# A retention layer and a gated MLP on one core: blocks of 256 rows, quarters of the array, a written program order

## The chip, the cores and the metric

The kernel runs on one core of a Trainium2 chip. A core has a matrix engine (TensorE; PE in the profile, its weight loads PEld), three engines for element-wise work (VectorE, DVE; ScalarE, ACT; GpSimd, POOL), and SyncE (SP), which here only issues DMAs. Each engine takes its instructions from its own queue in order, and waits in that queue for what other engines must have finished. The metric is the device time of one execution in microseconds (us); less is better. All times below are in us unless marked ns.

## The reference

Eight batches of 576 rows pass through a retention layer of eight heads of 64, and then through a gated MLP with a spatial gate (a mixing of the 576 rows with each other).

```python
scores = scale * np.matmul(q, k.transpose(0, 1, 3, 2))      # q, k, v: 8 x 8 x 576 x 64
gamma = 1.0 - 2.0 ** (-5.0 - np.arange(H))
Dmat = np.where(rel >= 0, gamma[:, None, None] ** rel, 0.0) # rel = t - s
x = np.matmul(scores * Dmat, v)                             # -> 8 x 576 x 512
h = gelu(x @ w_in)                                          # 512 -> 1024, tanh form
u, v = h[..., :512], h[..., 512:]
v_n = (v - mean) / np.sqrt(var + 1e-06) * g_ln              # over the 512 columns
v_s = np.einsum('ts,bsd->btd', w_sg, v_n) + b_sg[None, :, None]
out = x + (u * v_s) @ w_out                                 # float32
```

## The kernel before

The decay gamma^(t-s) splits into a factor of the row t and one of the row s, so the retention runs as a linear recurrence over chunks of rows: inside a chunk the masked scores (`sc`, then `ret`) are multiplied with the values, and what came before enters through a 64x64 state for each head (`zp` in PSUM, its copy `zbd` in SBUF).

The 4608 rows are cut into 36 chunks of 128. Two batches form a pair of nine chunks (`NT`); the middle chunk (`MID`, the fifth) holds the last 64 rows of one batch and the first 64 of the next. Queries, keys and values come in float32 with one row a partition, in pieces of 64 numbers (256 bytes). For each chunk:

- `load` (L67) issues the DMAs on SP; `prep` (L172) casts q and k to bfloat16 (L176) and multiplies v by its decay factor (L178), both on POOL.
- `attn_T` (L184) transposes q and k on PE, two heads on top of each other; DVE copies `qT` (L191), and ACT (L193) and DVE (L194) put the two heads of k into the halves of a zero-padded tile `kbd`, so that a whole 128x128 array computes the scores of one head.
- `attn_S` (L197) computes the scores and DVE multiplies them by the triangular mask (L208).
- `attn_O` (L212) sums the carried part (L223) and the local part (L228) in PSUM, each with half of the array's columns; DVE multiplies by the row's decay from the table `ttab` and writes `xT` (L231), which has the columns of x on the partitions.
- `attn_Z` (L234) adds to the state; DVE (L247) and ACT (L248) copy its diagonal blocks into `zbd`.
- `mlp_V` (L254): four matmuls of 512 columns (`hv`, L258), gelu on ACT (`vg`, L261), mean and variance on DVE (L263, L265), 1/sqrt(var) and -mean/sqrt(var) on POOL (L267, L268, L270), and the normalised `vn` on ACT (L272).
- `mlp_U` (L275): sixteen matmuls (`hu`, L282) and gelu into `uT` (L285).

For a batch whose five chunks of `vn` are there, `mlp_W` (L287) mixes the rows: for each of four groups of columns and each half of 288 rows five matmuls (`wp`, L295). DVE applies g and b in one instruction (`vs`, L301) and multiplies by `uT` in a second one (`gT`, L304). Then for each chunk `mlp_O` (L306) does the last matmuls (L311), adds x through a matmul with the identity (L314), copies to SBUF (`ob`, L317), and issues the output DMA from ACT's queue (L318).

The loop at L354 names the order of this work: for step i the scores of chunk i, the MLP of chunk i-1, the transposes of chunk i+1, and two waiting pieces of `mlp_W` and `mlp_O` a step. A planner may still reorder each engine's queue by data and priorities. PSUM has eight banks: one each for transposes, `ot` and the state, two for scores, three (`psD`) for `hv`, `hu`, `wp` and `op`.

Of the kernel before, what the change touches and what calls it, by code (L numbers as in the profile page):

```python
# [19 lines left out]
def kernel(  # L20
# [18 lines left out]
    NP = B // 2  # L39
# [11 lines left out]
    vnp = ctx.enter_context(tc.tile_pool(name="vnp", bufs=14))  # L51
# [5 lines left out]
    def segs(m):  # L57

        if m < MID:
            return [(0, 0, 128 * m, 128)]  # L60
        if m == MID:
            return [(0, 0, 128 * m, S - 128 * m), (S - 128 * m, 1, 0, 128 * (m + 1) - S)]
        return [(0, 1, 128 * m - S, 128)]
# [3 lines left out]
    def load(i):  # L67
        p, m = divmod(i, NT)
        qk = ld.tile([128, 2, H, D], F32, name="qk", tag="qk")
        vf = ld.tile([128, H, D], F32, name="vf")  # L70
        for (p0, b, r0, n) in segs(m):
            bb = 2 * p + b
            nc.sync.dma_start(qk[p0:p0 + n, 0, :, :], q[bb, :, r0:r0 + n, :].transpose([1, 0, 2]))
            nc.sync.dma_start(qk[p0:p0 + n, 1, :, :], k[bb, :, r0:r0 + n, :].transpose([1, 0, 2]))
            nc.sync.dma_start(vf[p0:p0 + n, :, :], v[bb, :, r0:r0 + n, :].transpose([1, 0, 2]))
        loaded[i] = (qk, vf)

    load(0)

# [5 lines left out]
    g_col = consts.tile([128, KK], F32, name="g_col")  # L85
    w_stage = []
    for half in (1, 0):
        for c in (0, 2):
            wst = ld.tile([128, 2, F2], F32, name="wst", tag="qk")
            nc.sync.dma_start(wst[:], moe_w_in.rearrange("(c p) f -> p c f", p=128)[:, c:c + 2, half * F2:(half + 1) * F2])  # L90
            w_stage.append((half, c, wst))
        load(1 if half else 2)
    nc.sync.dma_start(b_bc[:], moe_b_sg.partition_broadcast(128))
    nc.sync.dma_start(g_col[:], moe_g_ln.rearrange("(c p) -> p c", p=128))


    ident = consts.tile([128, 128], BF, name="ident")
    make_identity(nc, ident[:])
    tri = consts.tile([128, 128], BF, name="tri")
    nc.gpsimd.memset(tri[:], 1.0)  # L100
# [306 lines left out]
```

## Time and profile before

| | |
|---|---|
| Median of three runs | 277.83 us (277.71 to 278.25) |
| Span of the profiled execution, first to last instruction | 276.5 us |
| Busy: PE / DVE / ACT / POOL | 232.7 / 197.4 / 128.1 / 121.9 us |
| Moved by DMA | 41.75 MB in 120,670 packets, 113,792 of them under 512 bytes |
| Mean granted TensorE clock | 0.963 |

The page gives the profiled execution by its span alone, which is 1.3 us under the median of the runs; a sum of its rows is a sum for the span. In a row of a group stand the line, the engine, the operation, out<-in with shapes, the count, then the busy time of the group and the mean ns of one, and after the second bar the idle time of the engine just before them with what ended it. In a row of the timeline stand the start and the length of a run of equal instructions. Matmuls are pipelined: one lasts about 0.22 us from start to end while the next may start after a quarter of that, so a rate is read from starts, and a busy PE isn't a PE at its peak.

### The profile page before, as it was taken

To read this page: it belongs to the slowest core of one execution; us is meant where nothing else is said; L and a number is where in the kernel's file an instruction comes from. 1 tells how busy PE (TensorE), PEld (TensorE's weight loads), DVE (VectorE), ACT (ScalarE), POOL (GpSimd) and SP (SyncE) were. 2 spreads that over 40 slices of the span, in tenths; PEclk is the share of its full clock that TensorE was granted. 3 is DMA by queue.
4 is the path that set the end of the run, shared out by engine and by line. 5 is a ranking of instruction groups with operands and counts; after the bars stand their busy time and mean duration, and the time that the engine had idled before them with its cause. 6 is when DMAs were issued, how large, how long until landed. Compare 5 with 4: busy or idle time off the path is not lost.

```text
span 276.5 us, 6611 instructions
## 1 busy us (share of the span) xinstructions
PE 232.7 (84%) x2626; PEld 167.1 (60%) x2626; DVE 197.4 (71%) x446; ACT 128.1 (46%) x226; POOL 121.9 (44%) x204
## 2 busy tenths in 40 slices
PE   0376894989999889988899799888997999989794
PEld 0234663666757666666666566666666776666562
DVE  4444663579997898569966996679876975698170
ACT  3441443242446445563455355562555456644603
POOL 4924417057445364546625485364555551111200
PEclk9995797599999999999999999999999999999999
DMA  8999899987005899879829996999658002200214
GB/s 173 256 280 207 163 210 202 223 162 163 10 2 146 205 211 202 185 161 244 162 92 225 183 209 154 210 187 181 147 148 195 0 27 90 78 2 2 78 76 190
DMA packets 120670, 41.75 MB, mean 151 GB/s; under 512 B 113792, under 2 KB 114880, under 8 KB 120640
## 3 DMA queue, kind: packets, MB, share of 16 engines
q1 hardware_dynamic: 114272, 30.71, 55.7%
q10 hardware_dynamic: 5184, 9.44, 9.2%
q0 software_dynamic: 1184, 1.19, 2.5%
q8 instruction: 20, 0.33, 0.5%
q14 instruction: 10, 0.08, 0.1%
HBM read 33.08 MB, written 9.44 MB: 154 GB/s over the span
## 4 chain that ended last, share of the span: by engine, by line
DVE 41%; PE 25%; ACT 10%; DMA 7%; issue 6%; POOL 6%; ACTq 2%; SPq 2%; POOLq 0%; DVEq 0%
DVE ret L208 8%; DVE vs L301 8%; DVE gT L304 7%; DMA wst<-in_moe_w_in_dram 6%; DVE bst L263 5%; PE op L311 5%; DVE xT L231 5%; ACT ob L317 5%; PE hv L258 4%; PE hu L282 4%; PE wp L295 3%; ACT vg L261 3%; PE tp L189 2%; ACTq L318 2%; POOL rs L268 2%
## 5 line engine op out<-in xcount | busy, mean ns | idle before, releaser
L267 POOL TENSOR_SCALAR rs<-mv 128x1 f32<-128x1 f32 x36 | 8.0, 223 | 113.3 <-DVE mv L265 106.1
L272 ACT ACTIVATE vn<-vg,nm,rs 128x512 bf16<-128x512 f32 x36 | 29.3, 814 | 52.3 <-POOL nm L270 52.3
L282 PE MATMUL hu<-xT,w_in 128*128 128x128 bf16 x576 | 40.5, 226 | 6.5 <-DVE w_in L349 3.2
L208 DVE TENSOR_TENSOR ret<-sc,tri 128x512 bf16<-128x512 f32 x64 | 40.9, 680 | 6.1 <-PE sc L206 6.0
L263 DVE BATCH_NORM_STATS2 bst<-vg 128x6 f32<-128x512 f32 x36 | 24.7, 687 | 27.6 <-ACT vg L261 27.6
L176 POOL CAST qkb<-qk 128x1024 bf16<-128x1024 f32 x36 | 37.5, 1041 | 14.6 <-DMA qk<-in_k_dram 9.6
L295 PEld LDWEIGHTS <-vn 128*128 128x128 bf16 x320 | 30.0, 97 | 20.3 <-issue 13.0
L258 PE MATMUL hv<-w_in,xT 128*128 128x512 bf16 x144 | 39.9, 399 | 2.7 <-DVE xT L231 2.5
L282 PEld LDWEIGHTS <-w_in 128*128 128x128 bf16 x576 | 36.3, 101 | 9.5 <-issue 4.8
L311 PE MATMUL op<-w_out,gT 128*128 128x512 bf16 x144 | 37.2, 379 | 0.0
L261 ACT ACTIVATE vg<-hv 128x512 f32<-128x512 f32 x36 | 21.5, 596 | 28.1 <-PE hv L258 22.1
L301 DVE SCALAR_TENSOR_TENSOR vs<-wp,g_col,b_bc 128x288 bf16<-128x288 f32 x64 | 29.8, 504 | 4.0 <-PE wp L295 4.0
L189 PE MATMUL tp<-ident,qkb 128*128 128x128 bf16 x288 | 24.3, 232 | 9.6 <-POOL qkb L176 9.6
L189 PEld LDWEIGHTS <-qkb 128*128 128x128 bf16 x288 | 20.6, 104 | 17.9 <-POOL qkb L176 9.8
L285 ACT ACTIVATE uT<-hu 128x512 bf16<-128x512 f32 x36 | 21.3, 591 | 14.4 <-PE hu L282 14.4
L317 ACT ACTIVATE ob<-op 128x512 f32<-128x512 f32 x36 | 20.9, 592 | 12.6 <-PE op L314 9.5
L231 DVE TENSOR_TENSOR xT<-ot,ttab 128x512 bf16<-128x512 f32 x36 | 24.4, 677 | 1.8 <-PE ot L228 1.3
L304 DVE TENSOR_TENSOR gT<-vs,uT 128x288 bf16<-128x288 bf16 x64 | 25.5, 436 | 0.0
L191 DVE COPY qT<-tp 128x512 bf16<-128x512 bf16 x36 | 14.9, 415 | 12.5 <-PE tp L189 12.2
L268 POOL TENSOR_TENSOR rs<-rs,mhalf 128x1 f32<-128x1 f32 x36 | 20.6, 571 | 2.8
L258 PEld LDWEIGHTS <-xT 128*128 128x128 bf16 x144 | 12.6, 100 | 12.8 <-DVE xT L231 3.7
L311 PEld LDWEIGHTS <-gT 128*128 128x128 bf16 x144 | 12.5, 98 | 9.0
(104 smaller groups left out, 383.3 us busy)
## 6 DMA issues: line engine op xcount, KB each, us to landing
out_dram<-ob ACTq DMA_DIRECT2D x36, 256.0 KB, 2.4
qk<-in_q_dram SPq DMA_DIRECT2D x32, 256.0 KB, 4.8
qk<-in_k_dram SPq DMA_DIRECT2D x32, 256.0 KB, 4.8
vf<-in_v_dram SPq DMA_DIRECT2D x32, 256.0 KB, 5.0
wst<-in_moe_w_in_dram SPq DMA_DIRECT2D x4, 512.0 KB, 7.6
qk<-in_q_dram SPq DMA_DIRECT2D x8, 128.0 KB, 4.1
qk<-in_k_dram SPq DMA_DIRECT2D x8, 128.0 KB, 4.2
vf<-in_v_dram SPq DMA_DIRECT2D x8, 128.0 KB, 4.3
```

The source lines that it names most:

```text
L176: nc.gpsimd.tensor_copy(qkb[:], qk[:].rearrange("p a h d -> p a (h d)"))
L189: nc.tensor.transpose(tp[:, a, kk, :], s["qkb"][:, a, kk * 128:(kk + 1) * 128], ident[:])
L208: nc.vector.tensor_tensor(ret[:, 4 * j:4 * j + 4, :], sc[:], msk[:].unsqueeze(1).to_broadcast([128, 4, 128]), op=Alu.mult)
L231: nc.vector.tensor_tensor(xTs[p][:, :, 128 * m:128 * m + 128], ot[:], ttab[:, :, t0:t0 + 128], op=Alu.mult)
L258: nc.tensor.matmul(hv[:], xTs[p][:, kk, 128 * m:128 * m + 128], w_in[:, kk, F2:], start=(kk == 0), stop=(kk == KK - 1))
L263: nc.vector.bn_stats(bst[:], vg[:])
L282: nc.tensor.matmul(hu[:, c, :], w_in[:, kk, 128 * c:128 * c + 128], xTs[p][:, kk, 128 * m:128 * m + 128], start=(kk == 0), stop=(kk == KK ...
L295: nc.tensor.matmul(ps[half][:], vns[t0 + j][:, 128 * c:128 * c + 128], wT[e][j][:, half * HS:(half + 1) * HS], start=(j == 0), stop=(j == ...
L301: nc.vector.scalar_tensor_tensor(vs[:], ps[half][:], g_col[:, c:c + 1], b_bc[:, half * HS:(half + 1) * HS], op0=Alu.mult, op1=Alu.add)
L304: nc.vector.tensor_tensor(gTs[p][:, c, col:col + HS], vs[:], uTs[p][:, c, col:col + HS], op=Alu.mult)
L311: nc.tensor.matmul(op[:], gTs[p][:, c, r], w_out[:, c, :], start=(c == 0), stop=False, skip_group_check=True)
L317: nc.scalar.activation(ob[:], op[:], Act.Copy)
```

## The change

Rows are worked in 18 blocks of 256. A partition holds two neighbouring rows (index `a`), so that a piece of a load is 512 bytes; the two chunks of a block (`c`) lie on partitions 0 to 63 and 64 to 127. Scores, local part, carried part and state use quarters of the array: 64 contraction rows and 64 output columns, chosen by the partitions of the operands. So `kbd` and `zbd`, with their zeros, go, and the middle chunk's masks and state take 32-row slices.

The decay of the query row, with the 1/8, goes into the cast of q (`gq`), now a multiplication on POOL; `xT` is a plain copy on ACT. k is copied to `kT` by ACT, q to `qT` by DVE, each in one instruction a block. g enters where the mean is subtracted (`vc`, DVE), 1/sqrt(var) in `vn` on ACT. b enters through 64 rows of `vn` and `wT` of each batch that were zero: `vn` holds ones there (`vnm`) and `wT` holds b, split into three bfloat16 rows by `build_b`; so one DVE multiplication follows the mixing. `mlp_W` is split by halves of the rows. Output DMAs are issued from SP, the two stages of w_in from ACT.

Every engine issues in the order in which the program names its work (`manual_schedule`). `later` and `tick` put a chunk's statistics two pieces of work behind its `hv`, and its `vn` four; `spare` does one waiting piece of W or O, or two of the ten transposed parts of w_sg at the start. PSUM: four banks for transposes, scores, `ot` and `wT` (tag `att`), one for the state, three as before.

The core of the diff (lines that stay, the tables and the launch are left out):

```diff
-    ld = ctx.enter_context(tc.tile_pool(name="ld", bufs=5))
-    work = ctx.enter_context(tc.tile_pool(name="work", bufs=4))
+    ld = ctx.enter_context(tc.tile_pool(name="ld", bufs=3))
+    w2 = ctx.enter_context(tc.tile_pool(name="w2", bufs=2))
+    w3 = ctx.enter_context(tc.tile_pool(name="w3", bufs=3))
-    psA = ctx.enter_context(tc.tile_pool(name="psA", bufs=1, space=bass.MemoryType.PSUM))
-    psS = ctx.enter_context(tc.tile_pool(name="psS", bufs=2, space=bass.MemoryType.PSUM))
+    psA = ctx.enter_context(tc.tile_pool(name="psA", bufs=4, space=bass.MemoryType.PSUM))
+    psZ = ctx.enter_context(tc.tile_pool(name="psZ", bufs=1, space=bass.MemoryType.PSUM))
+    ctx.enter_context(tc.manual_schedule())
...
+    def load(j):
+        qk = ld.tile([128, 2, H, 2, D], F32, name="qk")
+        vf = ld.tile([128, H, 2, D], F32, name="vf")
...
+                nc.sync.dma_start(
+                    dst[p0:p1], src[b, :, s0:s0 + hi - lo, :].rearrange("h (p a) d -> p h (a d)", a=2))
...
+    def build_b():
...
+        nc.vector.tensor_copy(bh[:], b_bc[:])
+        nc.vector.tensor_scalar(bacc[:], bh[:], one[:, 0:1], None, op0=Alu.mult)
+        nc.vector.tensor_tensor(br[:], b_bc[:], bh[:], op=Alu.subtract)
+        for n in (1, 2):
+            bh = w2.tile([128, S], BF, name="bh")
+            nc.vector.tensor_copy(bh[:], br[:])
+            nc.vector.scalar_tensor_tensor(bacc[:], bh[:], one[:, n:n + 1], bacc[:], op0=Alu.mult, op1=Alu.add)
...
+    def cast(j, part, eng):
...
+            eng.tensor_tensor(s["qb"][:].rearrange("p a h d -> p h a d"), qk[:, 0], bc(gq, j), op=Alu.mult)
...
+    def Sc(j, g):
...
+        sc = [psA.tile([128, 2, 2, 128], F32, name="sc", tag="att") for _ in range(2)]
+        for x in range(2):
+            kk = 2 * g + x
+            for a in range(2):
+                for r in range(2):
+                    for c in range(2):
+                        rr, cc = slice(64 * r, 64 * r + 64), slice(64 * c, 64 * c + 64)
+                        nc.tensor.matmul(sc[r][cc, x, a, :], kT[rr, a, kk, cc], qT[rr, :, kk, cc],
+                                         start=True, stop=True, skip_group_check=True)
...
+    def Z(j, c):
...
+        for a in range(2):
+            for kk in range(KK):
+                for r in range(2):
+                    h = 2 * kk + r
+                    nc.tensor.matmul(z[64 * r:64 * r + 64, kk, :], s["kb"][rows, a, h, :], s["vb"][rows, a, h, :],
...
+        zb = w3.tile([128, KK, D], BF, name="zb")
+        nc.vector.tensor_copy(zb[:], z[:])
...
+    def inter(j):
...
+                for r in range(2):
+                    rr = slice(64 * r, 64 * r + 64)
+                    nc.tensor.matmul(ot[c][rr, kk, :, :n], zbs[2 * j + c][rr, kk, :],
+                                     qT[rr, :, kk, 64 * c:64 * c + n],
...
+    def intra(j):
...
+        for kk, a in ks:
+            for c in range(2):
+                for r in range(2):
+                    cc = slice(64 * c, 64 * c + 64)
+                    nc.tensor.matmul(ot[c][64 * r:64 * r + 64, kk], vb[cc, a, 2 * kk + r, :],
+                                     ret[cc, r, kk, a, :],
...
-        nc.vector.tensor_tensor(xTs[p][:, :, 128 * m:128 * m + 128], ot[:],
-                                ttab[:, :, t0:t0 + 128], op=Alu.mult)
+            nc.scalar.copy(xTs[p][:, :, 128 * m:128 * m + 128].rearrange("p k (t a) -> p k a t", a=2), ot[c][:])
...
-        nc.gpsimd.tensor_scalar(nm[:], mv[:, 0:1], rs[:], -1.0, op0=Alu.mult, op1=Alu.mult)
-        nc.scalar.activation(vn[:], vg[:], Act.Identity, scale=rs[:], bias=nm[:])
+            nc.vector.scalar_tensor_tensor(vc[:], vg[:], mv[:, 0:1], g_bc[:], op0=Alu.subtract, op1=Alu.mult)
...
+                nc.scalar.mul(vn[:], vc[:], rs[:])
...
+        later(2, stats)
+        later(4, norm)
...
-            nc.vector.scalar_tensor_tensor(vs[:], ps[half][:], g_col[:, c:c + 1],
-                                           b_bc[:, half * HS:(half + 1) * HS],
-                                           op0=Alu.mult, op1=Alu.add)
-            nc.vector.tensor_tensor(gTs[p][:, c, col:col + HS], vs[:], uTs[p][:, c, col:col + HS], op=Alu.mult)
+        nc.vector.tensor_tensor(gTs[p][:, c, col:col + HS], ps[:], uTs[p][:, c, col:col + HS], op=Alu.mult)
...
-        nc.scalar.dma_start(outf[128 * i:128 * i + 128, :], ob[:])
+        nc.sync.dma_start(outf[128 * i:128 * i + 128, :], ob[:])
...
+    cast(2, "q", nc.gpsimd)
+    cast(2, "k", nc.gpsimd)
+    cast(2, "v", nc.gpsimd)
+    build_b()
     load(3)
+    load(4)
...
+    for j in range(NB):
+        nx = j + 1 < NB
+        if j + 5 < NB:
+            load(j + 5)
+        intra(j)
+        if nx:
+            Sc(j + 1, 0)
+            Z(j + 1, 0)
+        if j + 3 < NB:
+            cast(j + 3, "q", nc.gpsimd)
+        spare()
+        spare()
+        V(2 * j)
+        spare()
+        U(2 * j)
+        if j + 2 < NB:
+            T(j + 2, "q")
+        if nx:
+            inter(j + 1)
+            Sc(j + 1, 1)
+            Z(j + 1, 1)
+        V(2 * j + 1)
+        if j + 3 < NB:
+            cast(j + 3, "k", nc.gpsimd)
+            cast(j + 3, "v", nc.gpsimd)
+        spare()
+        U(2 * j + 1)
+        if j + 2 < NB:
+            T(j + 2, "k")
+        spare()
+        spare()
+        release(2 * j)
+        release(2 * j + 1)
```

More of the change, by code (lines that the diff above doesn't have):

```diff
@@ L187, in attn_T, with T @@
+    def T(j, part):
+        s = blk[j]
+        src = s[part + "b"]
+        tp = psA.tile([128, 2, KK, 128], BF, name="tp", tag="att")
         for a in range(2):
             for kk in range(KK):
[L189 to L193 removed]
@@ L376 @@
+    while pend:
+        tick()
     run(len(wo))
```

422 lines of the change are left out of this document (216 added, 206 removed).

## The prediction, made before the change was run

> **What bounds the kernel now.** I read the page's totals and its chain of waits first, then the groups by line, then the timeline of two chunks in the middle, the hidden-projection matmuls (hv) over the run, and the DMA queues.
>
> ```profile
> span 276.5 us, 6611 instructions
> PE 232.7 (84%) x2626; PEld 167.1 (60%) x2626; DVE 197.4 (71%) x446; ACT 128.1 (46%) x226; POOL 121.9 (44%) x204
> DVE 41%; PE 25%; ACT 10%; DMA 7%; issue 6%; POOL 6%; ACTq 2%; SPq 2%; POOLq 0%; DVEq 0%
> ```
>
> No engine is full; the chain runs over DVE and PE in turn. PE's busy time overlaps itself, so its work is counted by starts. The timeline:
>
> ```profile
> 119.94 1.04 PE L258 MATMUL hv<-w_in,xT 128*128 128x512 bf16 x4 [0.37 <-DVE xT L231]
> 121.26 1.06 PE L282 MATMUL hu<-xT,w_in 128*128 128x128 bf16 x16
> 122.25 0.41 PE L223 MATMUL ot<-qT,zbd_160 128*64 128x128 bf16 x8
> 122.50 0.39 PE L228 MATMUL ot<-ret,vsc_153 128*64 128x128 bf16 x8
> 122.82 0.40 PE L244 MATMUL zp<-vsc_153,qkb 128*128 128x128 bf16 x4
> 123.63 0.41 PE L295 MATMUL wp<-wT_1_169,vn 128*128 128x288 bf16 x2
> ...
> 126.68 0.61 DVE L304 TENSOR_TENSOR gT<-vs,uT 128x288 bf16<-128x288 bf16 x2
> 127.29 1.03 POOL L176 CAST qkb<-qk 128x1024 bf16<-128x1024 f32 x1
> 128.07 1.48 DVE L304 TENSOR_TENSOR gT<-vs,uT 128x288 bf16<-128x288 bf16 x2
> 128.30 1.09 POOL L178 TENSOR_TENSOR vsc_157<-vf,gv 128x512 bf16<-128x512 f32 x1
> ```
>
> One 128x128 matmul spans about 0.22, so 16 hu in 1.06 start every 0.056; hv every 0.216; wp every 0.122; the half-width ot matmuls, 8 in 0.41, every 0.028: the two column halves run side by side. The last hu starts at 122.10 and the first ot at 122.25: 0.15 instead of 0.056, so a change of array form costs 0.095; from ot to zp the same.
>
> Per block of 256 rows (two chunks) PE must start: transposes 16 x 0.056 = 0.90, scores 0.90, ot 32 x 0.028 = 0.90, state 8 x 0.056 = 0.45, hv 1.73, hu 1.79, wp 17.8 x 0.122 = 2.17, op 2.18 (8 of 512 columns at hv's pace, 8 of 128), four form changes 0.38: 11.4.
>
> ```profile
> L258 PE MATMUL hv<-w_in,xT x144: 376/379/634, 15.6 to 256.9; 128*128 128x512 bf16 x144
> 0.00:50.00 50.00, 5.77 (x16) 0.84 1.02 213
> 50.00:257.00 207.00, 33.82 (x128) 0.99 0.63 139
> 50.98 1.03 PE L258 MATMUL hv<-w_in,xT 128*128 128x512 bf16 x2 [0.15 <-DVE xT L231]
> 256.26 1.03 PE L258 MATMUL hv<-w_in,xT 128*128 128x512 bf16 x4
> 262.08 0.28 PE L295 MATMUL wp<-wT_0_173,vn 128*128 128x288 bf16 x1 [1.49 <-ACT ob L317]
> 273.18 0.34 ACTq L318 DMA_DIRECT2D out_dram<-ob  x1
> ```
>
> Four hv groups (16 matmuls) lie before 50, 32 behind. From chunk 4 (50.98) to chunk 35 (256.26) a block takes 205.3 x 2 / 31 = 13.25: about 1.85 of PE stall. First hv 15.6, end of span 20.2 behind the last.
>
> **The change part by part.**
>
> ```profile
> L208 DVE TENSOR_TENSOR ret<-sc,tri 128x512 bf16<-128x512 f32 x64 | 40.9, 680 | 6.1 <-PE sc L206 6.0
> L301 DVE SCALAR_TENSOR_TENSOR vs<-wp,g_col,b_bc 128x288 bf16<-128x288 f32 x64 | 29.8, 504 | 4.0 <-PE wp L295 4.0
> L304 DVE TENSOR_TENSOR gT<-vs,uT 128x288 bf16<-128x288 bf16 x64 | 25.5, 436 | 0.0
> L263 DVE BATCH_NORM_STATS2 bst<-vg 128x6 f32<-128x512 f32 x36 | 24.7, 687 | 27.6 <-ACT vg L261 27.6
> L231 DVE TENSOR_TENSOR xT<-ot,ttab 128x512 bf16<-128x512 f32 x36 | 24.4, 677 | 1.8 <-PE ot L228 1.3
> L191 DVE COPY qT<-tp 128x512 bf16<-128x512 bf16 x36 | 14.9, 415 | 12.5 <-PE tp L189 12.2
> L194 DVE COPY kbd_158<-tp 64x512 bf16<-64x512 bf16 x18 | 7.7, 428 | 1.8 <-ACT kbd_158 L193 1.3
> L193 ACT ACTIVATE kbd_158<-tp 64x512 bf16<-64x512 bf16 x18 | 10.5, 585 | 9.3 <-DVE qT L191 9.3
> L248 ACT ACTIVATE zbd_160<-zp 64x256 bf16<-64x256 f32 x16 | 6.1, 380 | 5.2 <-DVE zbd_160 L247 4.9
> L317 ACT ACTIVATE ob<-op 128x512 f32<-128x512 f32 x36 | 20.9, 592 | 12.6 <-PE op L314 9.5
> L176 POOL CAST qkb<-qk 128x1024 bf16<-128x1024 f32 x36 | 37.5, 1041 | 14.6 <-DMA qk<-in_k_dram 9.6
> L178 POOL TENSOR_TENSOR vsc_155<-vf,gv 128x512 bf16<-128x512 f32 x7 | 7.3, 1040 | 0.1
> L268 POOL TENSOR_TENSOR rs<-rs,mhalf 128x1 f32<-128x1 f32 x36 | 20.6, 571 | 2.8
> L267 POOL TENSOR_SCALAR rs<-mv 128x1 f32<-128x1 f32 x36 | 8.0, 223 | 113.3 <-DVE mv L265 106.1
> L272 ACT ACTIVATE vn<-vg,nm,rs 128x512 bf16<-128x512 f32 x36 | 29.3, 814 | 52.3 <-POOL nm L270 52.3
> L247 DVE CAST zbd_160<-zp 64x256 bf16<-64x256 f32 x16 | 6.6, 411 | 2.0 <-PE zp L244 1.8
> L265 DVE BATCH_NORM_AGGREGATE mv<-bst 128x2 f32<-128x6 f32 x36 | 6.3, 176 | 0.9
> ```
>
> DVE. The decay multiply on xT goes (24.4) and becomes a copy on ACT (36 x 0.59 = 21.3). kbd's DVE half goes (15.4 over both buffers); kT is one ACT copy of 1024 columns a block: 0.585 for the first 512, and 0.42 for 512 more (256 more cost 0.21 between zbd's 0.380 and ob's 0.592), 1.01. qT is one copy of 1024: 0.415 plus about half as much again for a second 512 without its fixed part, 0.68 instead of 0.83. vs and gT (55.3) become one multiply out of PSUM: 0.45 (0.68 at 512 columns less 224 of them), 28.7 in all. New: the centring with g (vc), 36 times, 512 f32 columns out of two SBUF operands; between 0.59 and 0.74, I take bst's 0.69: 24.8. DVE: 197.4 - 24.4 - 15.4 - 2.7 - 26.6 + 24.8 = 153, plus some 8 at the start: 8.9 a block instead of 10.9. ACT gains xT, loses zbd's half (12.2 over both buffers), and vn keeps its 0.81 or less, for it has one pointer operand fewer, with eight half-height pieces on the four middle chunks (+3): under 8 a block, hidden by PE. The added b costs nothing per block: it rides in rows of the middle chunks' vn and wT that were zero; its price is build_b, below. Zeroing kbd and zbd, the tables ttab and tri, and kmid go; all lay in the start or beside other POOL work. Output DMAs move from ACT's queue, where the issue took 0.34 behind ob, to SP's, where each now waits for its ob; behind it stand the next output and load j+5, whose tiles are cast two blocks later, so nobody waits: nothing, and it costs only if ob's three buffers run out while SP hands out a load.
>
> POOL. q's cast becomes a multiply, 1024 elements at vsc's pace, 2.0, k 1.04, v 2.0, and per chunk 0.22 + 0.57: 6.6 of a block of 12. Hidden, except for one thing: gT above, two SBUF operands, takes 0.61 a pair beside little POOL work and 1.48 beside the casts. The new gT reads PSUM, as vs does (504 throughout), and escapes; the centring does not. In program order q's cast ends long before the first centring, and k and v end about when the second begins: up to 0.5, which I take into the stall.
>
> PE. Scores: 32 quarters instead of 16 whole; ot's local part: 32 quarters for 16 halves; state: 32 of 64 columns for 8; carried part: 16 as before, two abreast, 0.45. No row shows row quarters. If four run in the time of a pair, 0.014 each; if starts are no denser than the densest here, 0.028. Below 0.014 nothing speaks for it: a pair already lasts its 128 columns. I take 0.020, nearer the low end, as the pairs show no cost for the second: 0.64 for each of the three. Block: 0.90 + 3 x 0.64 + 0.45 + 1.73 + 1.79 + 2.17 + 2.18 + 0.38 = 11.5. So PE gains nothing (bounds 10.9 and 12.3).
>
> The Trainium skill (TensorEngine Tiling (Array Packing), Key Properties) says that a change of tiling mode drains TensorE and a change of tile does not. The trace agrees on the first with its 0.15; it shows no change of row tile. The skill's TensorE: Matmul & The Clock Gate (Back-to-back issue gap) puts a floor near 25 ns under start to start; by it the three groups would be 0.80 each and the time about 8 more. The trace has nothing closer than its pairs, 0.028 a matmul, which neither break nor need that floor.
>
> Order. The written order puts a fixed queue on each engine, so I laid one block out by these rows. Transposes, scores, ot and wT share four att buffers. When the second half's scores start, ot holds two; of the other two, one was the q transpose's, and is free only when DVE has copied qT. DVE's queue before that copy is: two masks (1.36), the state copy (0.41), up to three gT (1.35), then bn_stats, its aggregate (0.18) and the centring (1.56 together), which wait for ACT's gelu. In a block with six W, qT is copied by 6.85 after the block's start, while PE, through two W, hv, W, hu, transposes and the carried part, is there at 5.8: it waits 1.1. In a block with four O, PE gets there at 7.2 and DVE, with no gT, is done at 7.6: 0.45. The other buffers turned out free in time: the three of psD (drained 1.5 or more before they are needed), the state's one, the two or three of each cast. Mean of both kinds 0.8; with 0.15 a block for the centring's wait, 0.95: 12.45 a block, against 13.25.
>
> Start.
>
> ```profile
> q1 hardware_dynamic: 114272, 30.71, 55.7%
> q10 hardware_dynamic: 5184, 9.44, 9.2%
> q0 software_dynamic: 1184, 1.19, 2.5%
> ```
>
> Per packet 0.557 x 16 x 276.5 / 114272 = 21.6 ns (256 bytes) and 78.5 ns (1.8 KB); 512 bytes then 31 ns, between 22 and 43. The pieces of 512 bytes halve the load packets: 107 us of DMA instead of 149, off the path in steady state. But build_b, on DVE, stands before block 0 and waits for b, which SP issues behind three blocks: 9 x 1024 x 31 / 16 = 17.9, w_in 5.4, broadcasts 1.4 (2 KB packets at about 85 ns), 2 until the first lands, POOL's queue (0.025 x 276.5) up to 6.9: b at 27 to 34; I take 31. build_b's ten instructions at 0.4 to 0.7: 6. Then masks and the first wT copies: 3, since PE waits there for att buffers. First hv at 40 instead of 15.6: the start gives back 24, and only the short blocks 0 to 2 behind it win that back (below), as before's chunks 0 to 4 took 35 (15.6 to 50.98) with transfers and casts in turn.
>
> Sum. There are 100 pieces of W (64) and O (36), six places for them in a block, none before block 3, and 14 left for the end. First hv 40; rest of block 0 with its wT builds 9, blocks 1 and 2 without pieces 8.5 each (DVE's 7.3 and PE's 7.2 plus the waits): 26; blocks 3 to 16: 14 x 12.45 = 174.3, less 4.3 for four empty places (0.85) and the last transposes (0.90); block 17 up to its second hv: local part, two pieces, hv, piece, hu: 5. From there: hv 0.86, hu 0.90, three pieces 2.55, 1 of wait for the last vn, 8 W x 0.61 and 6 O x 1.09 = 11.4, ob 0.6, and the 3.3 that lie between the last issue (273.18) and the end: 21, where before took 20.2. In all 262. The runs' median is 277.8, 1.3 above the profiled span of 276.5; with it 263.
>
> **The rivals.**
> - Quarters no denser than halves (0.028): three groups at 0.90, +0.8 a block, of which W blocks hide some: 274. For it: nothing denser is shown. Against: the second half is free now.
> - Same bank: in the carried part the two row quarters write one bank. If they go one by one, 16 x 0.056 instead of 8 x 0.056: +8, 271. Rows say nothing either way. The Trainium skill (TensorEngine Tiling (Array Packing), Gotcha 1: PSUM Pressure) says that row tiles cannot use one PSUM bank at once.
> - The other side: the centring finds POOL's casts running. It then waits for one, up to 2.0; qT's copy, the scores' masks and so PE stand behind it. With 1.4 a block: 263 + 25 = 288, slower. It decides from 0.8 a block (14.5 / 18). For it: 1.48 against 0.61 above. Against: POOL has 5 idle of 12 and the order keeps them apart.
> - The change doesn't do what it says: DVE's relief is not where PE waits, and stalls stay at 1.85: +0.9 x 15 = 277, no change.
> - Each change of row quarter costs 0.095: 48 a block, +82: 345.
>
> **How the numbers follow.** Forecast 0.50 (own range 252 to 273), quarters 0.18, same bank 0.06, centring 0.15, no effect 0.08, row changes 0.03. Faster is the first three, 0.74; within 0.2% (0.55 us, what a measurement can tell) half of no effect, 0.04; slower 0.22. Time 263; range from the quarters' low bound and an earlier b (249) to the lighter half of the centring case (283).
>
> **What would show it.** Right, in the order of the steps: hv first near 40, then blocks near 12.4; DVE near 160 busy; quarters starting closer than 28 ns; xT on ACT near 0.6; the wait before the second scores put down to qT. Wrong: centring well over 0.7 with POOL beside it; quarters at 28 ns or more; b landing after 36; DVE or ACT waiting longest for each other in the written order.

## The result, and the profile after

The changed kernel takes 265.1 us (median; 264.3 to 265.7), the kernel before in the same comparison 277.8: ratio 0.955, 95% interval [0.952, 0.958]. It is 4.5% faster. The profiled execution took 265.4 with a span of 263.5.

The page of the changed kernel, its totals and the engines of the chain of waits:

```profile
span 263.5 us, 8276 instructions
PE 211.5 (80%) x3549; PEld 158.8 (60%) x3586; DVE 173.7 (66%) x343; ACT 135.8 (52%) x210; POOL 133.8 (51%) x143
q1 hardware_dynamic: 61920, 38.31, 57.3%
PE 58%; DVE 16%; SPq 9%; ACT 7%; DMA 5%; issue 4%; ACTq 0%; DVEq 0%
```

Before, DVE stood in the chain with 41%, PE with 25%, DMA with 7% and SP's issue of loads (SPq) with 2%. Now PE carries 58%; SPq with 9% and DMA with 5%, most of it b's transfer, lie mostly at the start. From the view of waits, PE alone:

```profile
PE wtp L169 <- DVE ret L244: 14.6, 1, 14.6
PE tp L217 <- DVE qb L199: 11.7, 2, 9.2
PE sc L239 <- DVE qT L222: 8.5, 13, 1.7
PE sc L239 <- ACT kT L224: 4.1, 4, 1.7
```

One single wait of 14.6 us lies at the start, ahead of the first hidden projection, and the 11.7 lie before that, for the first two casts of q; the 13 short ones are those of the second scores for q's transposed copy. The groups by line that answer to the terms of the sum:

```profile
L244 DVE TENSOR_TENSOR ret<-sc,mask 128x512 bf16<-128x512 f32 x72 | 46.3, 685 | 35.4 <-PE sc L239 35.3
L366 DVE TENSOR_TENSOR gT<-wp,uT 128x288 bf16<-128x288 f32 x64 | 27.5, 450 | 13.1 <-PE wp L363 12.8
L323 DVE SCALAR_TENSOR_TENSOR vc<-vg,mv,g_bc 128x512 f32<-128x512 f32 x36 | 27.4, 762 | 1.3
L222 DVE COPY qT<-tp 128x1024 bf16<-128x1024 bf16 x18 | 12.4, 687 | 1.4 <-PE tp L217 1.3
L302 ACT CAST xT<-ot 128x512 bf16<-128x512 f32 x36 | 23.9, 738 | 1.2 <-PE ot L294 1.2
L199 POOL TENSOR_TENSOR qb<-qk,gq 128x1024 bf16<-128x1024 f32 x16 | 30.9, 1933 | 1.2 <-DMA qk<-in_q_dram 1.2
L320 POOL TENSOR_SCALAR rs<-mv 128x1 f32<-128x1 f32 x36 | 24.8, 690 | 90.8 <-ACT uT L353 35.3
```

And one stretch of the timeline, in block 8, with the quarters on PE:

```profile
122.18 0.64 PE L294 MATMUL ot<-ret,vb 64*64 64x128 bf16 x32
122.66 0.39 PE L239 MATMUL sc<-qT,kT 64*64 64x128 bf16 x16
127.84 0.52 PE L282 MATMUL ot<-qT,zb 64*64 64x128 bf16 x12
128.15 0.24 PE L239 MATMUL sc<-qT,kT 64*64 64x128 bf16 x1
128.20 0.28 PE L282 MATMUL ot<-qT,zb 64*64 64x128 bf16 x4
128.31 0.22 PE L239 MATMUL sc<-qT,kT 64*64 64x128 bf16 x1
128.69 0.41 PE L239 MATMUL sc<-qT,kT 64*64 64x128 bf16 x14 [0.17 <-DVE qT L222]
```

A quarter lasts 0.22. So 16 of them in 0.39 are four rounds of four with three steps of 0.057 between them ((0.39 - 0.22) / 3), and 32 in 0.64 seven steps of 0.06: four start together, then the next four, and one costs 0.014 to 0.015. The carried part (L282) starts every 0.027 (12 in 0.52): two at once, though both write one bank. The two single scores at 128.15 and 128.31 have found their buffer; the other 14 wait for qT.

The hidden projections (hv; some records of theirs are missing), with first and last start:

```profile
L308 PE MATMUL hv<-w_in,xT x110: 379/379/634, 44.2 to 244.0; 128*128 128x512 bf16 x110
```

Two of their rows in the timeline, the first of the run and chunk 4's:

```profile
44.17 1.49 PE L308 MATMUL hv<-w_in,xT 128*128 128x512 bf16 x3 [0.34 <-issue]
66.59 0.81 PE L308 MATMUL hv<-w_in,xT 128*128 128x512 bf16 x3 [0.20 <-issue]
```

The longest hv lasts 0.634 and the shortest 0.379, so the first ones start every 0.43 ((1.49 - 0.63) / 2) and those of chunk 4 every 0.216: behind the wait of 14.6, PE works at half pace. The windows of this trace give a granted clock of 0.50 from 33 to 48.4 and of 1.00 from 49 to 78.

The time by stretches, from the timeline's starts of hv and of the local part (L294: block 0's successors start at 55.8, 64.3 and 73.5, block 17 at 238.7; chunk 35's hv at 243.3), against the prediction's sum:

| stretch | predicted, us | measured, us |
|---|---|---|
| to the first hv | 40 | 44.2 |
| from there to the start of block 3 | 26 | 29.3 |
| blocks 3 to 16 (14) | 170 | 165.2 |
| block 17 up to its second hv | 5 | 4.6 |
| from there to the end | 21 | 20.2 |
| span | 262 | 263.5 |

The total is off by 1.5, but through two misses that cancel: the start was taken 7.5 us too short, the rest 6 too long.

Against the kernel before, with the rows that the prediction shows: chunk 4's hv starts at 66.6 instead of 51.0, so the start gives back 15.6. From there to chunk 35's hv it takes 176.7 instead of 205.3 (11.4 a block for 13.25), 28.6 less. The rest takes 20.2 in both.

### The profile page after: what moved, and what is told of

Same layout as the page of the kernel before. It is cut to its first block, busy times and chain, and to the rows that moved or that the text cites. A ratio compares the mean times of both kernels' runs of the same rounds, so it can differ in the third digit from the quotient of the medians.

```text
span 263.5 us, 8276 instructions
## 1 busy us (share of the span) xinstructions
PE 211.5 (80%) x3549; PEld 158.8 (60%) x3586; DVE 173.7 (66%) x343; ACT 135.8 (52%) x210; POOL 133.8 (51%) x143
## 3 DMA queue, kind: packets, MB, share of 16 engines
q1 hardware_dynamic: 61920, 38.31, 57.3%
## 4 chain that ended last, share of the span: by engine, by line
PE 58%; DVE 16%; SPq 9%; ACT 7%; DMA 5%; issue 4%; ACTq 0%; DVEq 0%
PE wp L363 14%; PE hv L308 12%; PE op L374 9%; SPq L71 7%; PE hu L350 7%; PE sc L239 4%; DVE vc L323 4%; DMA b_bc<-in_moe_b_sg_dram 3%; DVE bst L316 3%; DVE qT L222 3%; PE zp L264 3%; PE ot L294 3%; PE tp L217 3%; PE op L377 2%; SPq L89 2%
## 5 line engine op out<-in xcount | busy, mean ns | idle before, releaser
L244 DVE TENSOR_TENSOR ret<-sc,mask 128x512 bf16<-128x512 f32 x72 | 46.3, 685 | 35.4 <-PE sc L239 35.3
L209 POOL TENSOR_TENSOR vb<-vf,gv 128x1024 bf16<-128x1024 f32 x18 | 34.8, 1934 | 15.2 <-DMA vf<-in_v_dram 15.2
L363 PE MATMUL wp<-wT,vn 128*128 128x288 bf16 x256 | 40.8, 286 | 0.0
L366 DVE TENSOR_TENSOR gT<-wp,uT 128x288 bf16<-128x288 f32 x64 | 27.5, 450 | 13.1 <-PE wp L363 12.8
L335 ACT ACTIVATE vn<-vc,rs 128x512 bf16<-128x512 f32 x32 | 23.1, 722 | 18.5 <-POOL rs L321 15.1
L199 POOL TENSOR_TENSOR qb<-qk,gq 128x1024 bf16<-128x1024 f32 x16 | 30.9, 1933 | 1.2 <-DMA qk<-in_q_dram 1.2
L239 PE MATMUL sc<-qT,kT 64*64 64x128 bf16 x576 | 20.8, 224 | 12.8 <-DVE qT L222 8.5
L380 ACT COPY ob<-op 128x512 f32<-128x512 f32 x36 | 20.7, 585 | 15.7 <-PE op L377 13.6
L323 DVE SCALAR_TENSOR_TENSOR vc<-vg,mv,g_bc 128x512 f32<-128x512 f32 x36 | 27.4, 762 | 1.3
L302 ACT CAST xT<-ot 128x512 bf16<-128x512 f32 x36 | 23.9, 738 | 1.2 <-PE ot L294 1.2
L239 PEld LDWEIGHTS <-kT 64*64 64x64 bf16 x576 | 13.3, 108 | 15.9 <-issue 10.6
L321 POOL TENSOR_TENSOR rs<-rs,mhalf 128x1 f32<-128x1 f32 x36 | 20.4, 566 | 3.0
L217 PE MATMUL tp<-ident,qb 128*128 128x128 bf16 x144 | 11.8, 229 | 11.7 <-DVE qb L199 11.7
```

The costliest lines, as they stand in the source:

```text
L199: eng.tensor_tensor(s["qb"][:].rearrange("p a h d -> p h a d"), qk[:, 0], bc(gq, j), op=Alu.mult)
L209: eng.tensor_tensor(s["vb"][:].rearrange("p a h d -> p h a d"), vf[:], bc(gv, j), op=Alu.mult)
L239: nc.tensor.matmul(sc[r][cc, x, a, :], kT[rr, a, kk, cc], qT[rr, :, kk, cc], start=True, stop=True, skip_group_check=True)
L244: nc.vector.tensor_tensor(s["ret"][:, r, 2 * g:2 * g + 2], sc[r][:], msk[:].unsqueeze(1).to_broadcast([128, 2, 2, 128]), op=Alu.mult)
L323: nc.vector.scalar_tensor_tensor(vc[:], vg[:], mv[:, 0:1], g_bc[:], op0=Alu.subtract, op1=Alu.mult)
L363: nc.tensor.matmul(ps[:], vns[t0 + j][e][:, 128 * c:128 * c + 128], wT[e][j][:, half * HS:(half + 1) * HS], start=(j == 0), stop=(j == SB ...
```

## The experiments

All ratios are to the kernel before, run on the same chip beside it; its medians there lay between 277.5 and 278.1. Where I give a difference to the changed kernel, it is between medians, and the changed kernel was not run again beside these runs, so a difference under 1 us says little.

**Are four quarters abreast, and what does one cost?** First the order of the quarters: all of one row group before the other, instead of in turn.

```diff
-        for x in range(2):                    # scores; the local part likewise
-            for a in range(2):
-                for r in range(2):
-                    for c in range(2):
+        for r in range(2):
+            for x in range(2):
+                for a in range(2):
+                    for c in range(2):
```

> The changed kernel with another order of the loops in scores and local part: the two quarters of one row group next to each other, the row groups one after the other (r outside in the scores, c outside in the local part). Same instructions, same count. If four quarters run abreast because their row groups alternate: starts of these matmuls go from 14 ns to 28 ns in the mean, each of the two groups from 0.45 to 0.90 a block, 18 blocks: +16 us, of which waits for DVE may hide up to 5: 276 to 281 us. If the density comes from the queue of instructions and not from the row groups, or if PE is not what sets the end: 265 us as now.

Measured: 266.1 us, ratio 0.957 [0.954, 0.960]; the same as the changed kernel. The timeline of this run shows why the order counts for little:

```profile
109.69 0.72 PE L294 MATMUL ot<-ret,vb 64*64 64x128 bf16 x26
110.20 0.24 PE L239 MATMUL sc<-qT,kT 64*64 64x128 bf16 x2
110.25 0.22 PE L294 MATMUL ot<-ret,vb 64*64 64x128 bf16 x2
110.28 0.22 PE L239 MATMUL sc<-qT,kT 64*64 64x128 bf16 x2
110.30 0.22 PE L294 MATMUL ot<-ret,vb 64*64 64x128 bf16 x2
```

The scores (L239) come after the whole local part (L294) in the program, yet four of them start before its last matmuls. Each row group takes its own instructions in order, a pair of column quarters every 0.056 (110.25, 110.30), and the other group runs beside it. So the groups overlap in this order too, and the question of the price needs more quarters. Each score matmul twice:

```diff
-                        nc.tensor.matmul(sc[r][cc, x, a, :], kT[rr, a, kk, cc], ...
+                        for _ in range(2):
+                            nc.tensor.matmul(sc[r][cc, x, a, :], kT[rr, a, kk, cc], ...
```

> Each score matmul of a 64x64 quarter is issued twice in turn with the same result: 18 x 32 = 576 quarters more, and nothing else changes. If four quarters run abreast and a start costs 0.014 (the mean of the groups in the trace of after), the second ones cost 576 x 0.014 = 8 us where PE sets the pace: 270 to 274. By the 0.020 of the prediction 11.5: 276 to 278. By 0.028 (no denser than halves) 16: 280 to 283. If a repeat has to wait until its own quarter is free and the four don't mix, 0.052 each: 295. A rival for all of them: the waits in front of the second scores (8.5 + 4.1 us) and behind them (masks) take up part of it, and the time moves by less than 8: under 270.

Measured: 271.8 us, ratio 0.978 [0.976, 0.980]: 6.7 more than the changed kernel for 576 quarters, 0.012 us each. That is a little low, for the first hv came 1.2 sooner in this run (43.0); from there to the end it is 7.5 more, 0.013 each, and the blocks from chunk 6 to 32 take 12.27 instead of 11.82, 0.014 each. Line 240 is the score matmul here, in a row of the timeline and then in the groups by line:

```profile
111.50 0.62 PE L240 MATMUL sc<-qT,kT 64*64 64x128 bf16 x32
```

```profile
L240 PE MATMUL sc<-qT,kT 64*64 64x128 bf16 x1152 | 29.7, 225 | 16.2 <-DVE qT L222 10.1 <-ACT kT L224 5.3 <-issue 0.2
```

32 starts in 0.62 are again eight rounds with steps of 0.057, 0.014 each. The program names each quarter twice in turn, so two of a round should be the same quarter; how PE fits them in isn't shown. The time lies in the first case, 270 to 274; the prediction's 0.020 and all dearer values are out, and so is the rival that the waits take it up: the waits in front of the scores are no shorter (10.1 + 5.3 for qT and kT, 8.5 + 4.1 in the changed kernel).

**Where does the gain come from?** Four parts of the change, undone one at a time. First the copy to xT back on DVE:

```diff
-            nc.scalar.copy(xTs[p][:, :, 128 * m:128 * m + 128]...
+            nc.vector.tensor_copy(xTs[p][:, :, 128 * m:128 * m + 128]...
```

> The copy of ot to xT goes back from ACT to DVE, where the kernel before had it: 36 x about 0.69 = 25 us more on DVE (174 becomes 198, what it was before), 27 us less on ACT. If DVE's relief is where the time came from (PE waits for what DVE does in turn), the two copies of a block stand in DVE's queue ahead of the first masks of the next scores and of the state copy, 1.4 us a block: PE waits 0.8 to 1.4 more in 18 blocks, 278 to 290, the time of before and more. Rival (DVE has room, 11 of 12 us at most are filled, and PE does other work meanwhile): 264 to 270, the same within 2%.

Measured: 275.0 us, ratio 0.991 [0.987, 0.995]. 9.9 us of the 12.7 are gone with this one line, less than the 13 to 25 expected of it. DVE is back at 194.6 busy. The waits of PE that are new:

```profile
PE op L374 <- DVE gT L366: 4.5, 7, 0.7
PE wp L363 <- DVE gT L366: 2.4, 4, 0.6
```

They add up to 6.9. DVE comes later to the multiply with u, and by the program the next matmul then has no free buffer of psD. Chunk 6 to 32 go at 12.37 a block instead of 11.82. So taking this copy off DVE carries a large part of the gain, 0.55 us a block, and the rival that DVE has room for this copy is out.

Then the centring with g. Here POOL makes the negative mean, ACT makes vn from it as before, and g multiplies behind the mixing again; b's rows meet 1/g. Gelu's output `vg`, which now lives until vn, has three buffers instead of two:

```diff
-            vc = w3.tile([128, F2], F32, name="vc")
-            nc.vector.scalar_tensor_tensor(vc[:], vg[:], mv[:, 0:1], g_bc[:], op0=Alu.subtract, op1=Alu.mult)
+            nc.gpsimd.tensor_scalar(nm[:], mv[:, 0:1], rs[:], -1.0, op0=Alu.mult, op1=Alu.mult)
...
-        nc.vector.tensor_tensor(gTs[p][:, c, col:col + HS], ps[:], uTs[p]..., op=Alu.mult)
+        nc.vector.scalar_tensor_tensor(gTs[p][:, c, col:col + HS], ps[:], g_col[:, c:c + 1], uTs[p]...)
```

> One part of the change undone: no centring on DVE. POOL makes -mean x 1/std, ACT makes vn from gelu's output as before, and g multiplies per column in the product with u, where g was before; the spare rows of vn hold 1/g, so that b still comes out right. DVE loses 36 x 0.76 = 27 us and gains 64 x about 0.05; POOL gains 36 x 0.22 = 8. If the centring is what makes qT late (it stands ahead of the qT copy, 0.76 and its wait for the port a block twice), the wait for qT falls from 8.5 us to 2 or less and the time to 255 to 259. Rival (the masks and the state copy ahead of it, and POOL's rs, are what holds the qT copy, or PE gives it back a step later): 262 to 267.

Measured: 266.3 us, ratio 0.962 [0.958, 0.966], 1.1 above the changed kernel. Waits of PE in this run (L243 is the scores):

```profile
PE sc L243 <- ACT kT L228: 5.7, 4, 1.9
PE sc L243 <- DVE qT L226: 3.2, 13, 0.6
```

The wait for qT does fall, from 8.5 to 3.2, but kT's grows by 1.6, and the time does not follow: the first hv comes 3.0 later (47.2), behind a reciprocal of 3.35 us that only this version needs. From there to the end it is 2.4 shorter. So of the two theories the rival's number holds, and the first one's mechanism in part: with the centring's place on DVE empty, the wait for qT is shorter, but what it frees is about 2 us and not 8. So it isn't the sum of DVE's work that counts: with xT's copy DVE was busy for 20.9 more and that cost 9.9, and without the centring it was busy for 17.9 less (155.8) and that gave back about 2.

Then the loads in pieces of 256 bytes, as before:

```diff
-                nc.sync.dma_start(
-                    dst[p0:p1], src[b, :, s0:s0 + hi - lo, :].rearrange("h (p a) d -> p h (a d)", a=2))
+                for a in range(2):
+                    nc.sync.dma_start(
+                        dst[p0:p1, :, a, :], src[...].rearrange("h (p a) d -> p h a d", a=2)[:, :, a, :])
```

> Each load is split into its even and its odd rows, so that the pieces of a packet are 256 bytes as before instead of 512, with twice as many transfers on SP; everything else stays. If the transfers set the pace only at the start (theory), the blocks from 70 us on keep their 11.8 us and only the way to the first hidden projection grows: b, queued behind three blocks, lands later by 9 x 1024 pieces x (2 x 21.6 - 31) ns / 16 engines = 7 us, so 268 to 273. Rival (SP's longer list of issues and the longer transfers reach into the blocks, casts come late): 275 to 290, with POOL waiting for transfers all along. Third (pieces don't matter, the engines of the DMA wait anyway): 264 to 266.

Measured: 271.4 us, ratio 0.980 [0.975, 0.985], 6.3 more. The queue of the loads on the page, and hv with its first and last start:

```profile
q1 hardware_dynamic: 118368, 38.32, 68.0%
```

```profile
L309 PE MATMUL hv<-w_in,xT x144: 376/379/634, 48.5 to 250.5; 128*128 128x512 bf16 x144
```

4.3 of it is the first hv (48.5 instead of 44.2); the other 2 come behind it (from chunk 6 to 32, 13 blocks, 11.95 each instead of 11.82). The theory of the start holds for two thirds.

Last, the order written by hand against the scheduler's:

```diff
-    ctx.enter_context(tc.manual_schedule())
```

> The written order taken off: the scheduler places the same instructions by its own costs, as it did in the kernel before. Nothing of the work changes. If the order carries the gain (theory: the relief of DVE alone is worth little until the copies, masks and multiplies stand in the right place of its queue), the time goes back to 270 to 290, with PE's waits for masks and copies at 30 us or more in the steady part instead of 20. Rival (the work removed from DVE, ACT and the DMA engines carries it, the order is a detail): 262 to 268. A third way: the scheduler moves build_b, or the work that waits for it, out of the way of the first hidden projections, so that the start is shorter than 44 us and the time falls under 262 whatever the blocks do.

Measured: 269.5 us, ratio 0.968 [0.966, 0.970], 4.3 more: below the first theory's 270, above the rival's 268. The third case came true for the start alone, not for the time. Its first hv is early, at 33.6, but DVE then has build_b and the wT copies between its other work until 46.5, and the hv of chunk 6 starts at 77.6, to the tenth where the written order has it. Blocks from there take 12.06 instead of 11.82. So the early start was lost again by block 3, and the written order is worth some 4 us in the blocks and at the end. The four parts, undone alone, add up to 21.6 (9.9, 1.1, 6.3, 4.3), more than the 12.7, which is what is left after the loss at the start; whether they simply add isn't shown. What the quarters bring against the whole arrays of before was not run; the prediction's sum with 0.014 has 0.5 a block for them (10.9 for 11.4).

**What holds the start?** b's transfer ahead of the loads 1 and 2:

```diff
+    nc.sync.dma_start(b_bc[:], moe_b_sg.partition_broadcast(128))
     load(1)
     load(2)
     nc.sync.dma_start(g_bc[:], moe_g_ln.partition_broadcast(128))
-    nc.sync.dma_start(b_bc[:], moe_b_sg.partition_broadcast(128))
```

> The changed kernel, with the DMA of b issued ahead of the loads of blocks 1 and 2 instead of behind them. If the first hv (44.2 us) waits for b: b lands near 15 instead of 34.6, build_b starts when DVE has done its part of w_in (27.3), the first hv comes near 36 to 38 and the whole takes 257 to 259. If the transfers of the blocks or the transposed parts of w_sg hold the start, the first hv stays near 44 and the time at 265.

Measured: 256.5 us, ratio 0.923 [0.919, 0.926], 8.6 less than the changed kernel. The first row is of the chain of waits of the changed kernel:

```profile
25.56 9.06 DMA b_bc<-in_moe_b_sg_dram
```

The next rows are of the run with b ahead, the wait that was 14.6 and the start of hv:

```profile
PE wtp L169 <- DVE ret L244: 6.1, 1, 6.1
L308 PE MATMUL hv<-w_in,xT x110: 379/379/634, 35.7 to 235.0; 128*128 128x512 bf16 x110
```

The 8.5 us of the wait are the 8.5 of the first hv and those of the time: nothing behind gives them back. Then build_b too was called sooner, ahead of block 1's casts:

> As the one with b ahead, and build_b named before the casts of block 1, where DVE is idle. If build_b itself is on the path to the first hv: first hv near 30 (then held by w_in and by the first xT at 26.8), 250 to 253 us. If only the landing of b counted: as with b ahead, 257 to 259. If build_b delays block 1's q cast so that the start is held by that: above 259.

Measured: 259.6 us, ratio 0.934 [0.929, 0.938], 3.1 worse than without: the third case, with block 1's cast of q at 30.7 instead of 20.4 and the first hv at 39.8. DVE and POOL in this run's timeline:

```profile
22.41 4.38 DVE L153 TENSOR_SCALAR bacc<-bh,one 128x576 bf16<-128x576 bf16 x1
22.81 1.92 POOL L209 TENSOR_TENSOR vb<-vf,gv 128x1024 bf16<-128x1024 f32 x1
24.70 1.92 POOL L199 TENSOR_TENSOR qb<-qk,gq 128x1024 bf16<-128x1024 f32 x1
```

An instruction that takes 0.37 elsewhere ends 0.17 after the second of two POOL casts: it was held through both. Then the opposite, with b ahead: only the two wT tiles with rows of b need build_b, so they are built last and build_b is called in front of them, inside block 0:

```diff
-    build_b()
     load(3)
...
+            if len(wb) == 2:
+                build_b()
             for _ in range(2):
                 build_wT(*wb.pop(0))
```

> b's transfer ahead of the loads 1 and 2 (as in the run that moved b alone, 256.5 us), and the two wT tiles that hold rows of b are built last of the ten, with build_b in front of them instead of in front of block 0. If the first hidden projection waits for build_b alone, it falls from 35.7 us in that run to about 30, behind the w_in cast that ended at 27.2, and the time to 250 to 253. Rival (build_b's 6 us of DVE only move into block 0, where the masks and copies wait for them): 254 to 258, with the first hidden projections early and the later ones of the first three blocks where they were.

Measured: 260.7 us, ratio 0.942 [0.937, 0.946]; a miss: 4.2 worse than b ahead alone. The first hv is at 30.2, as expected, but block 3's at 73.8 instead of 69.1. Rows of DVE and POOL in the timeline, and a wait of PE:

```profile
34.72 2.08 DVE L323 SCALAR_TENSOR_TENSOR vc<-vg,mv,g_bc 128x512 f32<-128x512 f32 x1
41.92 2.05 DVE L151 CAST one<-ident 64x3 f32<-64x3 bf16 x2
42.02 1.93 POOL L209 TENSOR_TENSOR vb<-vf,gv 128x1024 bf16<-128x1024 f32 x1 [1.45 <-DMA vf<-in_v_dram]
45.57 2.07 DVE L157 CAST bh<-br 128x576 bf16<-128x576 f32 x1
```

```profile
PE tp L217 <- DVE wT L171: 3.3, 1, 3.3
```

Two of build_b's instructions and one centring stretch to the length of a POOL cast. build_b takes 8.5 us there (41.9 to 50.4) instead of 6 in the run with b ahead alone (27.2 to 33.2), and PE's next transposes wait behind it. The rival was right that the work only moves, and too mild on its price.

**The wait for qT.** The transposes of the next q go behind the second hidden projection, so that the second scores no longer meet their buffer:

```diff
         U(2 * j)
-        if j + 2 < NB:
-            T(j + 2, "q")
         if nx:
             inter(j + 1)
             Sc(j + 1, 1)
             Z(j + 1, 1)
         V(2 * j + 1)
+        if j + 2 < NB:
+            T(j + 2, "q")
```

> The changed kernel with the q transposes of block j+2 named behind the second hv instead of before the carried part, so that the second half's scores need no buffer that waits for the qT copy. If that wait (8.5 us in all in the waits of the changed kernel) is PE time lost: 257 us, and no wait of sc on qT. If the wait only moves (the transposes then wait for the masks, or the scores for something else on DVE): 263 to 267.

Measured: 267.9 us, ratio 0.963 [0.960, 0.967], slower than the changed kernel by 2.8. In the waits qT is gone, and another stands there; below it ACT's own wait for vn, 3.3 in the changed kernel:

```profile
PE sc L239 <- ACT kT L224: 12.6, 12, 1.6
ACT vn L335 <- DVE gT L366: 8.8, 7, 1.5
```

T also counts the delayed work forward (`tick`). With T moved, vn of the second chunk came one step sooner in ACT's queue, ahead of the kT copy, and waited there for DVE while kT stood behind it. So the same move once more, with the tick left at the old place:

> The transposes of the next q go behind the second hidden projection, as in the run with q's transposes later, but the place at which the delayed norm work is counted stays where it was, so that vn keeps its place behind the kT copy on ACT. Theory (the second scores wait for qT's copy, 8.5 us in all, and the earlier run only handed that wait to kT by the moved norm): the wait for qT goes and the wait for kT stays near 4: 256 to 261. Rival (PE gives the time back a step later, to kT's copy, the masks or vc, since DVE does the same work in the same block): 263 to 268, with the wait under another name.

Measured: 253.1 us, ratio 0.911 [0.909, 0.914], 12.0 less than the changed kernel. All that PE waits for ahead of the scores, and hv's first and last start:

```profile
PE sc L240 <- ACT kT L224: 3.4, 4, 1.1
```

```profile
L309 PE MATMUL hv<-w_in,xT x144: 379/379/634, 43.6 to 232.6; 128*128 128x512 bf16 x144
```

qT's 8.5 are gone and nothing took their place. The hv of chunk 6 comes 3.6 sooner (74.0 for 77.6), and the 13 blocks from there to chunk 32 take 11.2 each instead of 11.8: 7.8 more. That is the 11.4 between the spans (263.5 and 252.1). It is more than the 8.5. A part may be the clock: behind the longest of the 13 waits, 1.7 at 176.9, the changed kernel's PE again ran at half pace (granted 0.53 from 178 to 180), and hv, hu and eight transposes took 3.8 from 177.5 on instead of 2.1 in block 2. This run's trace has a granted clock of 1.00 there. No run separates the two.

**Together.** b ahead, rows of b last, transposes later with the tick kept:

> Three edits together: b's transfer ahead, the rows of b built last, q's transposes behind the second hidden projection with the place of the norm work kept. If each saves what it saves alone (8.6 by b, 12.0 by the transposes, 0 to 6 by the rows), 238 to 245; PE's own work at its start pace is 11 us a block, so the blocks can't fall under 198 us for 18 and the time not under 235. Rival (they share one stall: the first three blocks, which the transposes' move already shortened by 3 us): 246 to 250.

Measured: 249.8 us, ratio 0.901 [0.897, 0.906]: the fastest of all, 15.3 below the changed kernel, and short of the 238 to 245 expected. The time lies in the rival's 246 to 250, but its shared stall isn't there: the hv of chunk 6 comes at 70.3, 3.5 sooner than with the rows last alone (73.8), where the transposes' move alone gave 3.6 (74.0 for 77.6), and the blocks from there take 11.2 as in that run. The two add up. What falls short are the rows built last, as above: with b ahead alone the hv of chunk 6 came at 69.1, with the rows last at 73.8. b ahead with the transposes' move, without the rows, wasn't run; 8.6 + 12.0 would make it 244.5 if they add up.

## Why the prediction came out as it did

- **Quarters on PE.** The step took 0.020 between the bounds 0.014 and 0.028 and said that PE gains nothing, 11.5 a block for 11.4. Measured: 0.014, the low bound. With the three groups at 32 x 0.014 = 0.45 instead of 0.64 the sum gives 10.9. This term was mis-sized, by 0.6 a block, more than the difference between 12.14 (170 / 14) and 11.80 a block. PE's idle time was less than the 0.95 taken too: 7.5 in the 13 blocks from chunk 6 to 32, 0.6 each. 10.9 and 0.6 make 11.5; the last 0.3 is not accounted for. The reason given for the low end, that the second of a pair shows no cost, held for the row groups too.
- **DVE's relief and xT on ACT.** Right in kind: moving xT back alone returns 9.9 us. The size was off: DVE is busy for 173.7, not 153 and some 8. The centring is 2.6 more, and beside POOL's casts in the start a cast of w_in took 4.00 instead of 1.01 and a copy of build_b 2.07 instead of 0.46; the other 5 are not broken down. ACT's copy took 0.738, not 0.59, 0.15 more than ob's copy of as many; it differs in that it writes every other element, which no run tests. The hidden projections waited for it twice, 0.6 in all.
- **The wait for qT.** Predicted 1.1 in a block with six W, 0.45 in one with four O, from the order of DVE's queue. Measured 8.5 in 13 waits, between 0.2 and 1.7; from chunk 6 to 32 it is 5.6 in 10 waits, 0.4 a block where 0.8 was taken. Removing it freed 12. The wait and its cause were right, its size about twice too large in the blocks; that a step of the order could remove it for nothing the prediction did not see.
- **The centring.** Taken at 0.69, measured 0.762 in the mean, and its row (shortest, median, longest in ns) shows that it rarely meets a cast, as the order was read:

```profile
L323 DVE SCALAR_TENSOR_TENSOR vc<-vg,mv,g_bc x36: 750/751/1122, 48.8 to 246.1; 128x512 f32<-128x512 f32 x36
```

  It does hold POOL up: rs, issued beside it, takes 0.690 instead of 0.223, and 0.222 in the run without the centring.
- **The start.** b was put at 27 to 34, taken 31; it landed at 34.6. The packet price was mis-sized: the 31 ns of 512 bytes are about 36 (57.3% of 16 x 263.5 is 2,416 us; less 4,608 output packets at 78.5 ns, over the other 57,312). build_b took 7.0 instead of 6, for a POOL cast stretched one of its copies to 2.07. The rest of block 0 was put at 9 and took 11.6 (44.2 to 55.8). In block 1, which has no wT builds, it is 6.8 (57.5 to 64.3), so the step left 2.2 for them. They are 30 transposes behind the first hv, 1.0 for every ten and 1.5 for the first ten, 3.5 in all; and hv and hu ran at half pace, 0.9 and 0.7 more. The prediction has no term for the clock behind a long wait. Block 2 was 0.7 over (64.3 to 73.5), with a wait of 0.8 for kT (65.7) that block 1 doesn't have.
- **The rivals.** Quarters no denser than halves: out (0.014). Same bank: out (0.027 for the carried part). The Trainium skill (TensorEngine Tiling (Array Packing), Gotcha 1: PSUM Pressure) had said that row tiles cannot use one bank at once; here two that write different partitions of one bank did. The Trainium skill's floor of about 25 ns between starts (TensorE: Matmul & The Clock Gate, Back-to-back issue gap) does not hold across row quarters either; each row group alone keeps 0.056 a pair. The slower case, a centring behind POOL's casts, exists as a mechanism (2.08 in the run with the rows of b last) and hardly happens in this order. A cost of 0.095 for a change of row quarter: out, with 0.014 from start to start where rows change at every second matmul. No effect: out, by the run with xT on DVE.

So the forecast was right in its main steps, and close in its number because the quarters and the waits, cheaper than taken, paid for the longer start. That the two misses are of a size is luck.

## What to carry to other kernels

When work is moved off a full engine, lay out the next engine's queue step by step and ask which copy is late next: here that list named the next wait, and a step that removed it was worth 12.0 us where the whole change was worth 12.7. A constant that the first block needs should be loaded before the blocks that nobody needs yet. And a call that also counts delayed work moves two things: look at both when it is put elsewhere.

## What the runs showed of the hardware

- Behind its long wait at the start PE ran at half pace, and the granted clock does not always tell. In the changed kernel the first hv start every 0.43 instead of 0.216 behind a wait of 14.6, at a granted clock of 0.50. In the run with b ahead, behind a wait of 6.1, the windows give 1.00 from 33 to 40, and the first hv are as slow:

```profile
35.69 1.49 PE L308 MATMUL hv<-w_in,xT 128*128 128x512 bf16 x3 [0.33 <-issue]
```

- Matmuls on different row groups start out of program order: scores at 110.20 before local matmuls at 110.25 that stand ahead of them in the program. Each group of rows keeps its own order.
- A DVE instruction that meets two POOL casts back to back does not get in between them: a bf16 scaling took 4.38 instead of 0.37 in the run with build_b called sooner, and w_in's cast in the changed kernel 4.00 where its like took 1.01. The rows are of that kernel's timeline, DVE first and then POOL:

```profile
21.52 1.01 DVE L422 CAST w_in<-wst 128x1024 bf16<-128x1024 f32 x1
23.34 4.00 DVE L426 CAST w_in<-wst 128x1024 bf16<-128x1024 f32 x1
...
22.97 1.92 POOL L209 TENSOR_TENSOR vb<-vf,gv 128x1024 bf16<-128x1024 f32 x1
24.86 1.92 POOL L199 TENSOR_TENSOR qb<-qk,gq 128x1024 bf16<-128x1024 f32 x1
```

- The Trainium skill (SBUF — State Buffer, Who interferes with whom) has the two engines share a port that one takes for a whole instruction. These rows agree, and add that POOL's second cast went ahead of the DVE instruction that was already waiting.
